# Pairs of attention scores at other slots of two FFN tiles, and the raw weights of plain tiles at other slots

## The chip, the core and the metric

The kernel runs on one core of a Trainium2 chip. A core has a tensor engine (PE in the profile, with its weight loads as PEld), a vector engine (DVE), a scalar engine (ACT), a general engine (POOL) and a queue that issues DMAs (SP). Each works through its own list of instructions in order and waits on semaphores for the others. The metric is the device time of one execution in microseconds: the median of several runs, lower is better. The trace is that of one profiled execution.

## The reference

One transformer block over a sequence of 2048 tokens of width 576, in float32. Attention has 32 query heads of 18 and one shared key and value head; the FFN is gated and bilinear, 4608 wide:

```python
scores = einsum("bhqd,bkd->bhqk", q, k) * Dh ** -0.5
p = softmax(scores); o = einsum("bhqk,bkd->bhqd", p, v)
h = x + merge(o) @ wo               # x layer-normed before wq, wk, wv
g, u = ln(h) @ w_gate, ln(h) @ w_up
out = h + (g * u) @ w_down
```

Float32 products are made of fp32r products: each operand is split into a high part and the rest, and three of the four cross products are added.

## The kernel before, in words

The sequence is cut into four query blocks of 512. After a prologue, and the attention of the first block, the FFN of blocks 0, 1 and 2 runs (`ffn`, 36 tiles of the hidden width each, 108 in all), and between its matmuls the attention of the next blocks is worked in. The FFN of the last block has code of its own (`last_block`).

**A tile of the FFN** is 27 *slots*, counted by `j`. A slot is one matmul of the gate into the PSUM bank `pg` and one of the up product into `pu` (L1035); each uses 64 of the 128 rows of the array, so the two run side by side. Then ACT copies `pg` into `hf` (L1062), and DVE multiplies it by `pu` (L1067). Two tiles, an even and an odd one, make a *pair of tiles*: from their two `hf`, `left_first`, `left` and `left_sums` make the operands of the down product by a Strassen-like scheme of seven products (splits on POOL and DVE, lines L96 and L97, tiles `S` and `room`); the 42 matmuls of it (`down`, L987) run at the end of the *next* even tile. Their results are added to `h` by DVE (L993), or by an ACT copy to `tmp` (L997) and a POOL addition (L998).

**A pair of scores** (`pair`, with `scores`) is two matmuls side by side into a PSUM tile `s` (L701) and one ACT exponential of 128x1024 into `P` (L702). There are two `s` tiles, so a pair needs the exponential of the pair two before it. An FFN tile takes eight pairs while there are any (`on`). `flush` multiplies all `P` that wait with the values (L706); it runs at the end of every even tile, ahead of `down`. The order of all instructions is that in which the Python code makes them; no scheduler moves them. The list `PAIRS` names the slots ahead of which a pair stands: its first entry for even tiles, its second for odd ones, its third for the last tile of a block.

**Where the pairs stand before the change.** Even tile: ahead of slots 0, 4, 8, 12, 16 and 20, and two after the copy to `hf`. Odd tile: ahead of 0, 4, 8, 12, 16, 20 and 24, and one after the copy to `hf`. Then comes the next even tile, whose slot 0 has a pair again.

**The PSUM banks** of `pg`, `pu`, the down product and the output projection are handed out in turn from a ring of three (`ps_r`). An odd tile takes two; the next even tile takes the third for its `pg`, and for its `pu` the bank that was `pg` of the odd tile. So the first `pu` matmul of that even tile waits for the copy of the odd tile's `pg` to `hf`.

**Weights.** `load_w(n)` issues the DMA of the raw gate and up weights of tile n (`wr`, one buffer, 576 KB), and `split_w(n)` makes the high and low parts (`ws`, two buffers): a POOL cast and a DVE subtraction. Since `wr` has one buffer, the load of n+2 waits for the split of n+1.

**Plain tiles.** When the pairs are used up, tiles are not `on`: 15 tiles at the end of the FFN of block 2. They hold no pairs, `split_w` stands at slot 3 and `load_w` at slot 9, `down` comes ahead of the copy to `hf`, and steps of `ahead`, which prepare the last block, stand at some slots (`AHEAD`).

**Heads.** When the eight key-value passes of a group of heads are done, the result goes through DVE and through DMAs (`ob<-ob`) into the layout that the output projection wants. `run_aux`, at the end of a tile and at slot 12, makes these steps; one of them is an ACT cast of `ob` into `room` (L96), which waits for those DMAs.

Of the kernel before, what the change touches and what calls it, by code (L numbers as in the profile page):

```python
# [57 lines left out]
class Block:  # L58
# [951 lines left out]
    def ffn(self, b):  # L1010
        pe, act, dve = self.pe, self.act, self.dve
        X, hid, todo = self.X, [], None
        ahead = self.ahead()
        if b == 0:
            self.sums = self.weight_sums()
            next(self.sums)
        for f in range(NF):
            n_ = NF * b + f
            k = f % 2
            w = self.ws.pop(n_)  # L1020
            on = self.more(b + 2)
            last = f == NF - 1 and b + 1 < NB
            end = b == NB - 2
            if on:
                pg, pu = self.ps_r(f"pg{n_}"), self.ps_r(f"pu{n_}")
            else:
                gu = self.ps_s(f"gu{n_}")
                pg, pu = gu[:, 0], gu[:, 1]
            j = 0
            for c in range(9):  # L1030
                for wk, xk in ((0, 0), (0, 1), (1, 0)):
                    if on and j in (PAIRS[2] if last else PAIRS[k]) and self.more(b + 2):
                        self.pair()
                    for o, ps in ((0, pg), (64, pu)):
                        pe.matmul(ps, w[o:o + 64, wk, c], X[o:o + 64, xk, c], start=(j == 0), stop=(j == 26))  # L1035
                    if j == (8 if on else 2) and todo and not plain(n_ - 2):
                        self.left_sums()
                    if j == 3:
                        self.split_w(n_ + 1)
                    if j == (14 if on else 9):  # L1040
                        self.load_w(n_ + 2)
                    if j == 5 and k:
                        self.left_first(n_ - 1, hid[0])
                    if j == 12:
                        self.run_aux(within=True)
                    if 0 < f < NF - 1 and j in (8, 16, 24) and self.sums:
                        if next(self.sums, "end") == "end":
                            self.sums = None
                            self.load_wd(self.n_wd + 2)
                    if j == 6 and last and not end:  # L1050
                        self.normal(b + 1)
                    if end and f == TURN - 1 and j == 12:
                        self.normed[NB - 1] = self.mv, self.rstd(self.mv[:, :, 1], "bl", self.nc.gpsimd)
                    if end and f in AHEAD and j in AHEAD[f]:
                        for _ in range(AHEAD[f][j]):
                            next(ahead)
                    j += 1
            if todo and not on:
                drain(self.down(b, *todo))
                self.load_wd(self.n_wd + 7)  # L1060
            hf = self.hh.tile([P, TB], F32, tag="hf", bufs=2, name=f"hf{n_}")
            act.copy(hf, pg)  # L1062
            if on and not last:
                for _ in range(1 if k else 2):
                    if self.more(b + 2):
                        self.pair()
            dve.tensor_tensor(hf, pu, hf, ALU.mult)  # L1067
            hid.append(hf)
            if k:
                self.left(n_ - 1, hid)  # L1070
                hid = []
            if end and f in TURNS:
                for _ in range(TURNS[f]):
                    next(ahead)
            if not k or last:
                self.flush(len(self.pend))
            if todo and on:
                drain(self.down(b, *todo))
                self.load_wd(self.n_wd + 7)
            if f < NF - 1:  # L1080
                self.run_aux()
            todo = (f // 2,) if k else None
        if end:
            del X, pg, pu, gu, w, ps, hf, self.X
            self.last_block(ahead, self.down(b, *todo))
            return
        both(self.spread(b + 1), self.down(b, *todo))
        self.load_wd(self.n_wd + 4)
        if b + 2 < NB:
            self.load_x(b + 2)  # L1090
# [500 lines left out]
ORDER = (0, 3, 4, 2, 5, 6, 1)  # L1591
WD_BUFS = 9
NTMP = 3
PAIRS = (range(0, 24, 4), range(0, 28, 4), range(0, 24, 3))
AHEAD = {30: {4: 1}, 31: {3: 1, 7: 1, 11: 1, 15: 1, 19: 1, 23: 1}, 32: {4: 1},
         33: {3: 1, 7: 1, 11: 1, 15: 1, 19: 1, 23: 1}, 34: {10: 1}, 35: {5: 1, 11: 1, 17: 1, 23: 1}}
TURNS = {28: 5, 29: 2}
# [16 lines left out]
def both(a, b):  # L1614

    live = [a, b]
    while live:
        live = [x for x in live if next(x, drain) is not drain]


def plain(n):

    return n % NF == NF - 2
# [28 lines left out]
def drain(gen):  # L1652
    for _ in gen:
        pass
# [85 lines left out]
```

## Time and profile before

| what | value |
|---|---|
| median of 3 runs | 2316.66 us (2316.43 to 2317.4) |
| the profiled execution | 2313.73 us |
| its span in the trace | 2311.9 us |
| busy: PE, DVE, ACT, POOL | 98%, 58%, 61%, 39% of the span |
| FFN tiles with pairs | 93, from 372 to 1807 us of the span |
| plain tiles | 15, from 1820 to 1985 us |

A row of a timeline gives start and length in us, engine, line, operation, output<-inputs, shapes, and how many equal instructions it merges; in brackets stands the idle time of the engine ahead of it and what ended that. A row of the chain of waits gives start, length, and the engine and line that set the end at that time. A row of a waits view gives who waited for whom, the total in us, how many times, and the longest.

### The profile page before, as it was taken

What the parts mean: (1) busy time and instruction counts of PE and PEld (TensorE: products, weight loads), DVE (VectorE), ACT (ScalarE), POOL (GpSimd) and SP (SyncE); (2) the same over time, 40 slices, a digit from 0 to 9 for tenths busy, and PEclk for the clock granted to TensorE, in tenths of its full rate; (3) what the DMA queues carried; (4) which work ended last, traced back from release to release, by engine and by line L of the source; (5) the groups of instructions that cost most, each with busy time, mean ns of one, the idle gap of its engine ahead of it and who ended that gap; (6) DMA issues with size and microseconds to landing.
All of it is one profiled execution on the core that took longest, in us unless ns stands there. A gap on an engine that the chain in (4) does not pass through costs nothing.

```text
span 2311.9 us, 45915 instructions
## 1 busy us (share of the span) xinstructions
PE 2258.3 (98%) x17972; PEld 1660.3 (72%) x17972; DVE 1347.6 (58%) x2184; ACT 1418.9 (61%) x1902; POOL 897.6 (39%) x979
## 2 busy tenths in 40 slices
PE   7999999999999999999999999999999999999999
PEld 5333345777777777677777777777777778999999
DVE  8565645554545555455555456554454667778876
ACT  7888877656566665566665656665656412455553
POOL 4445302444443453334444444433333345322222
PEclk9999999999999999999999999999999999999999
DMA  5879834545554554645554554654333435677775
GB/s 175 272 253 302 276 122 118 163 146 169 168 158 153 168 169 146 195 147 165 155 166 147 171 172 144 178 180 143 124 121 99 138 129 170 190 252 246 228 246 178
DMA packets 200433, 407.01 MB, mean 176 GB/s; under 512 B 22637, under 2 KB 54509, under 8 KB 200213
## 3 DMA queue, kind: packets, MB, share of 16 engines
q1 hardware_dynamic: 197621, 393.42, 53.4%
q0 software_dynamic: 2592, 10.62, 1.5%
q8 instruction: 143, 2.34, 0.4%
q14 instruction: 77, 0.63, 0.1%
HBM read 317.27 MB, written 74.55 MB: 169 GB/s over the span
## 4 chain that ended last, share of the span: by engine, by line
PE 77%; DVE 3%; ACT 3%; POOL 2%; issue 2%; DMA 1%; SPq 0%; ACTq 0%; POOLq 0%; DVEq 0%
PE pg L1035 16%; PE acc L706 15%; PE y L987 12%; PE s L701 8%; PE gs L1253 8%; PE pu L1035 6%; PE yq L1218 4%; PE yo L832 3%; ACT P L702 2%; PE gu L1035 2%; PE gs L1260 1%; DVE ws L97 1%; PE y L957 1%; POOL h L998 1%; POOL room L96 1%
## 5 line engine op out<-in xcount | busy, mean ns | idle before, releaser
L702 ACT ACTIVATE P<-s 128x1024 f32<-128x1024 f32 x1024 | 1017.2, 1029 | 221.6 <-PE s L701 135.1
L1035 PE MATMUL pu<-X,ws 64*128 64x512 f32 x2511 | 680.0, 392 | 0.0
L1035 PE MATMUL pg<-X,ws 64*128 64x512 f32 x2511 | 674.7, 389 | 0.1
L1035 PEld LDWEIGHTS pg<-X,ws 64*128 64x128 f32 x2511 | 462.7, 186 | 46.1 <-ACT tmp L964 0.4
L706 PE MATMUL acc<-P,V 128*32 128x512 f32 x4096 | 479.9, 597 | 0.1
L1035 PEld LDWEIGHTS pu<-X,ws 64*128 64x128 f32 x2511 | 460.2, 186 | 25.0 <-ACT hf L1062 7.9
L701 PE MATMUL s<-q,kT 56*128 56x512 f32 x2048 | 438.7, 421 | 19.8 <-ACT P L702 18.6
L998 POOL TENSOR_TENSOR h<-h,tmp 128x288 f32<-128x288 f32 x306 | 239.4, 811 | 383.7 <-ACT tmp L997 382.4
L997 ACT COPY tmp<-y 128x288 f32<-128x288 f32 x306 | 122.1, 399 | 392.5 <-PE y L987 350.8
L701 PEld LDWEIGHTS s<-q,kT 56*128 56x128 f32 x2048 | 203.7, 184 | 200.5 <-ACT P L702 153.2
L987 PEld LDWEIGHTS y<-wdo,room 128*128 128x128 f32 x2142 | 294.9, 191 | 56.5 <-issue 36.2
L987 PE MATMUL y<-wdo,room 128*128 128x288 f32 x2142 | 309.6, 303 | 14.4 <-DVE h L993 11.4
L993 DVE TENSOR_TENSOR h<-h,y 128x288 f32<-128x288 f32 x408 | 175.3, 451 | 217.6 <-PE y L987 217.6
L706 PEld LDWEIGHTS acc<-P,V 128*32 128x32 f32 x4096 | 114.5, 109 | 260.6 <-issue 255.8
L97 DVE TENSOR_TENSOR ws<-wr,ws 128x1152 fp32r<-128x1152 f32 x108 | 190.1, 1760 | 129.4 <-POOL ws L96 126.6
L96 POOL CAST room<-hf 128x256 fp32r<-128x256 f32 (+1 forms) x108 | 68.4, 633 | 336.8 <-DVE hf L1067 336.8
L96 POOL CAST ws<-wr 128x1152 fp32r<-128x1152 f32 x108 | 128.7, 1192 | 135.7 <-DMA wr<-in_wgu_dram 135.7
L1067 DVE TENSOR_TENSOR hf<-pu,hf 128x512 f32<-128x512 f32 x93 | 63.8, 686 | 198.5 <-ACT hf L1062 198.5
L1201 POOL TENSOR_TENSOR wsum<-wsum,wsum 128x512 f32<-128x512 f32 x72 | 146.5, 2034 | 47.9 <-DMA wsum<-in_wgs_dram 38.9
L717 DVE STREAM_TRANSPOSE os<-acc 128x512 f32<-128x512 f32 x32 | 22.9, 717 | 149.5 <-PE acc L706 149.5
L1035 PE MATMUL gu<-X,ws 64*128 64x512 f32 x810 | 94.5, 389 | 0.0
L97 DVE TENSOR_TENSOR room<-hf,room 128x256 fp32r<-128x256 f32 (+1 forms) x108 | 90.7, 840 | 2.9 <-POOL room L96 2.9
(262 smaller groups left out, 2776.4 us busy)
## 6 DMA issues: line engine op xcount, KB each, us to landing
wdo<-wd_dram SPq DMA_DIRECT2D x492, 288.0 KB
wr<-in_wgu_dram SPq DMA_DIRECT2D x108, 576.0 KB
wsum<-in_wgs_dram SPq DMA_DIRECT2D x108, 256.0 KB
wd_dram<-wd_room SPq DMA_DIRECT2D x20, 1008.0 KB
wsum_dram<-wsum SPq DMA_DIRECT2D x72, 256.0 KB
raw<-wsum_dram SPq DMA_DIRECT2D x72, 256.0 KB
q<-q_dram SPq DMA_DIRECT2D x64, 216.0 KB
raw<-in_wgs_dram SPq DMA_DIRECT2D x54, 256.0 KB
```

The source lines that it names most:

```text
L96: (copy or self.cast)(hi, src)
L97: self.dve.tensor_tensor(lo, src, f32(hi), ALU.subtract)
L701: self.pe.matmul(s_[:, i], self.kT[o:o + 56, t * P:(t + 1) * P], q[o:o + 56, pr], start=True, stop=True)
L702: self.act.activation(p_, s_, AF.Exp, scale=SCALE)
L706: self.pe.matmul(acc[32 * j:32 * j + 32, :], self.V[:, t, :], Ps[j // 2][:, j % 2, :], start=(t == 0), stop=(t == NT - 1), skip_group_chec ...
L987: pe.matmul(y[:, :HD], m[:, t * P:(t + 1) * P], k, start=(first and j == 0), stop=(j == 2), skip_group_check=True)
L993: dve.tensor_tensor(hs, hs, y[:, :HD], ALU.add)
L997: act.copy(z, y[:, :HD])
L998: pool.tensor_tensor(hs, hs, z, ALU.add)
L1035: pe.matmul(ps, w[o:o + 64, wk, c], X[o:o + 64, xk, c], start=(j == 0), stop=(j == 26))
L1201: pool.tensor_tensor(to, x, y, op)
L1253: pe.matmul(bank[:, g * HT:(g + 1) * HT], W[:, wk, c, g], X[:, 2 * xk + c], start=(first and g == c == wk == xk == 0), stop=(c == 1 and wk ...
```

## The change

Three edits. In tiles with pairs, the even tile has them ahead of slots 3, 7, 11, 14, 18 and 22 and two after the copy to `hf`, as before in number; the odd tile has them ahead of slots 0, 4, 8, 11, 15, 19, 23 and 26, and none after the copy. In the last tile of a block they stand ahead of 0, 3, 7, 10, 13, 17, 20 and 23 instead of 0, 3, 6, ..., 21. The number of pairs in each tile is the same. In plain tiles, `split_w` of an even tile moves from slot 3 to slot 9, and `load_w` of an odd tile from slot 9 to slot 3.

```diff
-                    if j == 3:
+                    if j == (3 if on or k else 9):
                         self.split_w(n_ + 1)
-                    if j == (14 if on else 9):
+                    if j == (14 if on else 3 if k else 9):
                         self.load_w(n_ + 2)
...
             act.copy(hf, pg)
-            if on and not last:
-                for _ in range(1 if k else 2):
-                    if self.more(b + 2):
-                        self.pair()
+            for _ in range(2 if on and not k else 0):
+                if self.more(b + 2):
+                    self.pair()
             dve.tensor_tensor(hf, pu, hf, ALU.mult)
...
-PAIRS = (range(0, 24, 4), range(0, 28, 4), range(0, 24, 3))
+PAIRS = ((3, 7, 11, 14, 18, 22), (0, 4, 8, 11, 15, 19, 23, 26), (0, 3, 7, 10, 13, 17, 20, 23))
```

What this does to the order of instructions is shown at three places. The first is ACT around the end of odd tile 11; `P1_3_11_1` is the exponential of the eighth pair of that tile, `hf11` the copy, `P1_3_12_0` the first exponential of even tile 12. Before:

```order
L702 ACTIVATE P1_3_11_0_12396<-s1_3_11_0_12395 128x1024 [waits PE_49]
L1062 COPY hf11_12408<-pg11_12306 128x512 [waits DVE_49,PE_49]
L702 ACTIVATE P1_3_11_1_12411<-s1_3_11_1_12410 128x1024 [waits PE_49]
L702 ACTIVATE P1_3_12_0_12425<-s1_3_12_0_12424 128x1024 [waits PE_49]
L702 ACTIVATE P1_3_12_1_12441<-s1_3_12_1_12440 128x1024 [waits PE_49]
```

With the change:

```order
L702 ACTIVATE P1_3_11_0_12394<-s1_3_11_0_12393 128x1024 [waits PE_49]
L702 ACTIVATE P1_3_11_1_12407<-s1_3_11_1_12406 128x1024 [waits PE_49]
L1062 COPY hf11_12413<-pg11_12306 128x512 [waits DVE_49,PE_49]
L702 ACTIVATE P1_3_12_0_12431<-s1_3_12_0_12430 128x1024 [waits PE_49]
L702 ACTIVATE P1_3_12_1_12447<-s1_3_12_1_12446 128x1024 [waits PE_49]
```

The exponential of the eighth pair has moved ahead of the copy.

The second place is PE at the same boundary, from the last slot of tile 11 to the first of tile 12. Before:

```order
L1035 MATMUL pg11_12306<-X0_10336,ws11_12100 128x512
L1035 MATMUL pu11_12307<-X0_10336,ws11_12100 128x512
L701 MATMUL s1_3_11_1_12410<-q1_3_11313,kT_86 128x512 [waits Activation_49]
L701 MATMUL s1_3_11_1_12410<-q1_3_11313,kT_86 128x512
L701 MATMUL s1_3_12_0_12424<-q1_3_11313,kT_86 128x512 [waits Activation_49]
L701 MATMUL s1_3_12_0_12424<-q1_3_11313,kT_86 128x512
L1035 MATMUL pg12_12422<-X0_10336,ws12_12321 128x512 [waits DVE_49,Pool_49]
L1035 MATMUL pu12_12423<-X0_10336,ws12_12321 128x512 [waits Activation_49]
```

With the change:

```order
L701 MATMUL s1_3_11_1_12406<-q1_3_11311,kT_86 128x512 [waits Activation_49]
L701 MATMUL s1_3_11_1_12406<-q1_3_11311,kT_86 128x512
L1035 MATMUL pg11_12306<-X0_10336,ws11_12100 128x512
L1035 MATMUL pu11_12307<-X0_10336,ws11_12100 128x512
L1035 MATMUL pg12_12422<-X0_10336,ws12_12321 128x512 [waits DVE_49,Pool_49]
L1035 MATMUL pu12_12423<-X0_10336,ws12_12321 128x512 [waits Activation_49]
```

The two pairs between the tiles are gone; one now stands a slot earlier, the other three slots later. The wait of `pu12` for ACT has stayed.

The third place is DVE in plain tile 104, around the subtraction of `split_w` for tile 105 (`XS5` belongs to `ahead`, the `h2` row to `down`). Before:

```order
L97 TENSOR_TENSOR room_10399<-S_10400,room_10399 128x1024
L97 TENSOR_TENSOR ws105_28426<-wr105_28363,ws105_28426 128x1152
L1146 TENSOR_TENSOR XS5_28200<-xsums_28205,XS5_28200 128x512
L993 TENSOR_TENSOR h2_16912<-h2_16912,y2_15_0_28480 128x288
L993 TENSOR_TENSOR h2_16912<-h2_16912,y2_15_1_28481 128x288
```

With the change:

```order
L97 TENSOR_TENSOR room_10399<-S_10400,room_10399 128x1024
L1145 TENSOR_TENSOR XS5_28197<-xsums_28202,XS5_28197 128x512
L97 TENSOR_TENSOR ws105_28440<-wr105_28347,ws105_28440 128x1152
L993 TENSOR_TENSOR h2_16912<-h2_16912,y2_15_0_28480 128x288
L993 TENSOR_TENSOR h2_16912<-h2_16912,y2_15_1_28481 128x288
```

The subtraction for `ahead` and that of `split_w` have changed places. The same happens in tile 102. These are the only moves on DVE; on SP and POOL no instruction has another place than before.

## The prediction

> **What bounds the kernel now.** I read the page's busy line and its chain by engine first, then the chain in order of time over one pair of FFN tiles, then PE's waits and the waits on the copy to `hf`, and last the timelines of PE and ACT at one boundary between tiles.
>
> ```profile
> PE 2258.3 (98%) x17972; PEld 1660.3 (72%) x17972; DVE 1347.6 (58%) x2184; ACT 1418.9 (61%) x1902; POOL 897.6 (39%) x979
> PE 77%; DVE 3%; ACT 3%; POOL 2%; issue 2%; DMA 1%; SPq 0%; ACTq 0%; POOLq 0%; DVEq 0%
> ```
>
> PE is the bound; ACT has time to spare on average. The chain in order of time, from one flush to the next:
>
> ```profile
> 1747.63 7.00 PE acc L706 x64
> 1754.64 5.89 PE y L987 x42
> ...
> 1767.91 1.03 ACT P L702
> ...
> 1777.57 7.00 PE acc L706 x64
> ```
>
> A pair of tiles takes 1777.57 - 1747.63 = 29.94 us. Apart from PE one row of another engine is in it: at 1767.91 an exponential, at the boundary from the odd tile to the next even one. PE's waits over all tiles with pairs, and who waits for the copy to `hf`:
>
> ```profile
> PE s L701 <- ACT P L702: 15.0, 48, 4.4
> ...
>   PEld pu L1035: 7.9, 44
> ```
>
> The first row is what pairs wait for exponentials. The last says that 44 times the weight load of a `pu` matmul waits for the copy. 44 is the number of boundaries from an odd tile with pairs to an even one: 17 in each of the first two FFN blocks, 10 in the third. One of them on PE:
>
> ```profile
> 1767.47 0.39 PE L701 MATMUL s<-q,kT 56*128 56x512 f32 x2
> ...
> 1767.93 0.39 PE L1035 MATMUL pg<-X,ws 64*128 64x512 f32 x1
> ...
> 1768.16 0.39 PE L1035 MATMUL pg<-X,ws 64*128 64x512 f32 x1
> ...
> 1768.39 0.39 PE L701 MATMUL s<-q,kT 56*128 56x512 f32 x2
> 1768.98 0.50 PE L701 MATMUL s<-q,kT 56*128 56x512 f32 x2 [0.20 <-ACT P L702]
> 1769.32 0.39 PE L1035 MATMUL pg<-X,ws 64*128 64x512 f32 x1
> 1769.46 0.49 PE L1035 MATMUL pu<-X,ws 64*128 64x512 f32 x1
> ...
> 1770.73 0.39 PE L1035 MATMUL pg<-X,ws 64*128 64x512 f32 x1
> ```
>
> and on ACT:
>
> ```profile
> 1767.91 1.02 ACT L702 ACTIVATE P<-s 128x1024 f32<-128x1024 f32 x1
> 1768.83 0.58 ACT L1062 COPY hf<-pg 128x512 f32<-128x512 f32 x1
> 1769.29 1.05 ACT L702 ACTIVATE P<-s 128x1024 f32<-128x1024 f32 x1
> ```
>
> A slot takes 1768.16 - 1767.93 = 0.23 us, a pair's scores as much. From the last slot (1768.16) to the even tile's first `pu` (1769.46) are 1.30 us, in which PE has a slot and two pairs to do, 0.69: 0.61 us are lost. To slot 4 (1770.73) 1.27 us pass for four slots and a pair, 1.15: another 0.12, since `pg` and `pu` no longer start together. So about 0.73 us of each 29.94 us is loss, all here: 44 x 0.73 = 32 us is all that another placing could win at these boundaries.
>
> **The change part by part.** *Odd tile's end: the dear part.* The eighth pair now stands ahead of slot 26, and its exponential ahead of the copy on ACT. With the rows above as steps: scores start at 0; the exponential starts 0.44 later (1767.47 to 1767.91; the one of slot 23, three slots and a pair, 0.92 us, earlier, lets ACT go at the same moment, since the copy followed its exponential after 0.92); the copy starts 0.92 after that (1767.91 to 1768.83); the first `pu` of the even tile 0.63 after that (1768.83 to 1769.46). Sum 0.44 + 0.92 + 0.63 = 1.99. PE without a wait would be there after one pair and one slot, 0.46. Lost: 1.53 instead of 0.61, so **+0.92 us a boundary**; the 0.12 stay. The trace has no copy behind an exponential that late, so both ends: 0, if ACT took the copy right behind the exponential of slot 23 (0.92 earlier, a stall of 0.61 as now); and at most +1.2, if exponential and copy did not overlap (0.44 + 1.03 + 0.58, and 0.05 from the copy's end, 1769.41, to `pu`: 2.10, less 0.46) and the 0.12 came twice. I take 0.92, since the steps are all rows of the same boundary and ACT works in order.
>
> Queued behind the waiting `pu` are all of PE's even tile; on ACT nothing is delayed but the copy. The `hf` of the odd tile comes later with it, and DVE's and POOL's Strassen work too, but that is wanted only by `down`, after 27 slots and 7.00 us of `acc`.
>
> *Even tile's pairs later.* Slots 3 to 22 instead of 0 to 20 give the exponential two slots more at the start and take from the 7 slots ahead of the closing two pairs: 5 slots are 1.15 us, an exponential 1.03, so no new wait. The closing pairs, the flush, `down` and the start of the odd tile stay as they are.
>
> *The casts of heads.* Twelve times ACT has a cast for the output projection between the two tiles:
>
> ```profile
> L96 ACT CAST room<-ob 128x512 fp32r<-128x512 f32 x12 | 7.5, 626 | 7.1 <-DMA ob<-ob 7.0
> ...
> 431.16 7.00 PE acc L706 x64
> 462.23 7.00 PE acc L706 x64
> ...
> 525.32 7.00 PE acc L706 x64
> 555.18 7.00 PE acc L706 x64
> 585.56 7.00 PE acc L706 x64
> ...
> 678.45 7.00 PE acc L706 x64
> 708.64 7.00 PE acc L706 x64
> ```
>
> Here the first two exponentials of the even tile queue behind it. Against 29.86 us (525.32 to 555.18) the pairs of tiles with a cast take 31.07, 30.38 and 30.19: 1.2, 0.5 and 0.3 us more. Ten boundaries have these three sizes, two, two and six of them: 5.2 us. With the change PE gets to slot 3 later and has no pair before it; the cast fits. I take **-5 us**, between 0 and -5.2. The eleventh, at tile 38, is longer:
>
> ```profile
> 958.91 0.62 ACT L96 CAST room<-ob 128x512 fp32r<-128x512 f32 x1 [4.30 <-DMA ob<-ob]
> ...
> 960.50 0.80 PE L701 MATMUL s<-q,kT 56*128 56x512 f32 x2 [4.42 <-ACT P L702]
> ```
>
> The third pair of the tile waits for the first exponential. It stands ahead of slot 8 now and of slot 11 then: PE has three slots more behind it when the DMA lands, and the boundary's own stall goes under. **-0.7** there instead of +0.92.
>
> *Last tiles.* 3 or 4 slots apart instead of 3: nothing to win but some 0.1 us each; left out.
>
> *Plain tiles.* Both moved steps stand where they stood on SP and POOL: between slots 3 and 9 nothing else is queued there. So the DMA of `wr`, the cast and the subtraction begin when they began. On DVE two rows change places in tiles 102 and 104. In tile 104:
>
> ```profile
> 1947.49 2.13 DVE L97 TENSOR_TENSOR room<-S,room 128x1024 fp32r<-128x1024 f32 x1 [0.94 <-POOL room L96]
> 1949.55 1.35 DVE L97 TENSOR_TENSOR ws<-wr,ws 128x1152 fp32r<-128x1152 f32 x1
> 1950.82 1.27 DVE L1146 TENSOR_TENSOR XS<-xsums,XS 128x512 fp32r<-128x512 f32 x1
> 1952.02 0.81 DVE L993 TENSOR_TENSOR h<-h,y 128x288 f32<-128x288 f32 x2
> ```
>
> Both run back to back, and PE waits for the `h` row behind them; in the other order it starts at the same time. **0**, between -1.3 and +1.3 (one of the two rows).
>
> **Sum.** 43 x 0.92 = 39.6; -0.7; -5: **+34 us**. Against the profiled execution 2313.73 + 34 = 2347.7; that lies 2.9 under the median of the runs shown, against which I predict 2316.66 + 34 = **2350.7**. With the upper bound 43 x 1.2 - 0.7 - 5 = +46, 2363; with 0.75 a boundary +26.5, 2343. The likeliest's own range is 2343 to 2363.
>
> **Rivals.** *Faster: an evenly spread row of pairs keeps ACT busy and PE never waits.* For it: the 15.0 us of waits for exponentials, which the change goes at. It needs the copy to be off PE's path: the first `pu` would have to find another bank, or the copy to end within 0.46 us of the last scores. Against it: the 44 waits of `pu`, one at each boundary, and the change leaves the ring of banks as it is. Price: 44 x 0.73 + 5 = 37 won, 2279. Chance 0.07.
>
> *No change.* The lower bound above: the copy goes ahead of the last exponential or costs what it costs now. Then 0 to -5, 2312 to 2317. Against it is the order on ACT. Chance 0.05.
>
> *The clock.* PE stands still for 1.53 us a boundary, 1.14 of it idle (the even tile's first `pg` still runs, 0.39). What idle time did to the granted clock (in the last three rows, of a view by windows, it is the third number from the right):
>
> ```profile
> 1913.12 0.67 PE L987 MATMUL y<-wdo,room 128*128 128x288 f32 x3 [2.09 <-ACT tmp L997]
> ...
> 1952.51 2.84 PE L987 MATMUL y<-wdo,room 128*128 128x288 f32 x14 [2.35 <-DVE h L993]
> ...
> 960.30:963.70 3.40, 3.20 (x16) 2.55 (x18) 0.00 (x0) 2.26 (x4) 0.92 (x1) 0.51 0.93 300
> 1913.00:1915.40 2.40, 2.27 (x17) 2.11 (x17) 1.22 (x3) 1.19 (x4) 2.40 (x4) 1.00 0.65 216
> 1953.60:1957.00 3.40, 3.40 (x16) 3.40 (x15) 0.52 (x2) 1.59 (x4) 2.44 (x4) 0.50 0.70 211
> ```
>
> After 2.09 us of idling the clock stayed at 1.00, after 2.35 and 4.42 it fell to 0.50 for 3.4 us, which costs 1.7. If 1.14 us were enough, 44 x 1.7 = 75 more: 2425. By the rows they are not. Chance 0.04. The Trainium skill's page "TensorE: Matmul & The Clock Gate", section "A second HAM failure mode: psum-queue depth-cycling", speaks for this rival: a kernel whose matmul groups idle briefly at each turn of the PSUM banks went to and fro between the two clocks. By that rule the change costs far more than the stall. The same page's first part puts the fall after an idle window of some 3.4 us; the fall after 2.35 here is earlier than that.
>
> *The plain tiles do win.* If the raw weights came sooner, part of this idling would go:
>
> ```profile
> L987 PE MATMUL y<-wdo,room 128*128 128x288 f32 x297 | 48.5, 323 | 13.5 <-DVE h L993 11.4 <-ACT tmp L997 2.1
> ```
>
> All 13.5 and three half-clock stretches of 1.7: 18.6 less, 2332 together with the +34. Against it: PE waits here for DVE and ACT, none of it for `wr`, and the queues stand as they stood. Chance 0.06.
>
> **How the numbers follow.** Likeliest 0.78, clock 0.04, plain tiles 0.06: slower by over 0.2% (4.6 us, about what a measurement of this kernel can tell from no change) 0.88; same 0.05; faster 0.07. The range, 2326 to 2364, takes in the likeliest's own, its bounds and the plain-tile rival; left out are the faster, the same and the clock rival, 0.16.
>
> **What would show it.** In the changed trace: on ACT the row of `hf<-pg` 0.92 us behind the start of an exponential at each odd tile's end, with no other between it and the even tile's first `pu`; `PEld pu` waiting for it 44 times with 1.1 us or more each, 50 us in all, instead of 7.9; waits of `s` for `P` down from 15.0 to about 5; a pair of tiles at 30.8 us; the plain stretch from 1820 to 1985 as long as before. The prediction is wrong if `pu` waits no longer than now, if the clock is 0.5 in tiles with pairs other than 38, or if the plain stretch changes by over 2 us.

## The result, and the profile after

The changed kernel takes 2346.0 us (median of 4 runs, 2344.61 to 2346.59) where the kernel before, run beside it, takes 2316.55 us (4 runs, 2315.48 to 2317.4). The ratio is 1.0127, with a 95% interval of 1.0109 to 1.0144: the change costs 29 us. 2350.7 was predicted. The profiled executions differ by 2346.18 - 2313.73 = 32.4 us, against the predicted sum of 34.

The page of the changed kernel, its busy line, its chain by engine and the group of `pu` matmuls, with that group before behind it:

```profile
PE 2252.1 (96%) x17972; PEld 1655.2 (71%) x17972; DVE 1344.5 (57%) x2184; ACT 1419.6 (61%) x1902; POOL 896.6 (38%) x979
...
PE 73%; DVE 4%; ACT 3%; issue 3%; POOL 3%; DMA 1%; SPq 0%; ACTq 0%; POOLq 0%; DVEq 0%
...
L1035 PE MATMUL pu<-X,ws 64*128 64x512 f32 x2511 | 694.9, 392 | 51.5 <-ACT hf L1062 51.4
```

```profile
L1035 PE MATMUL pu<-X,ws 64*128 64x512 f32 x2511 | 680.0, 392 | 0.0
```

PE works no longer than before (2252.1 us against 2258.3); it stands still for longer. Before, its `pu` group had 0.0 us of idle time ahead of it, now 51.5. PE's waits in the tiles with pairs:

```profile
PE pu L1035 <- ACT hf L1062: 51.4, 44, 1.4
PE s L701 <- ACT P L702: 2.8, 1, 2.8
```

and, from the view of the copy's line, who waits for it:

```profile
  PEld pu L1035: 70.0, 44
```

The waits of pairs for exponentials are gone but for one (15.0 us before, 48 times), and each of the 44 boundaries now has a wait of `pu` that averages 51.4 / 44 = 1.17 us. The 70.0 us are the wait of the weight loads ahead of these matmuls; PE itself still has the first `pg` to do in a part of it and stands idle for 51.4. One boundary, on PE:

```profile
1800.72 0.39 PE L701 MATMUL s<-q,kT 56*128 56x512 f32 x2
...
1802.71 0.50 PE L1035 MATMUL pu<-X,ws 64*128 64x512 f32 x1 [1.14 <-ACT hf L1062]
...
1803.05 0.40 PE L1035 MATMUL pu<-X,ws 64*128 64x512 f32 x1
...
1803.29 0.39 PE L701 MATMUL s<-q,kT 56*128 56x512 f32 x1
...
1803.53 0.40 PE L701 MATMUL s<-q,kT 56*128 56x512 f32 x1
```

on ACT, the exponential of slot 26 and the copy:

```profile
1801.16 1.02 ACT L702 ACTIVATE P<-s 128x1024 f32<-128x1024 f32 x1
1802.08 0.58 ACT L1062 COPY hf<-pg 128x512 f32<-128x512 f32 x1
```

and what the chain of waits has at this boundary and the one before, with the copy of the odd tile in it (the exponential that the chain names is that of slot 23):

```profile
1769.40 0.94 ACT P L702
...
1771.24 0.59 ACT hf L1062
...
1780.21 7.00 PE acc L706 x64
...
1800.23 0.94 ACT P L702
...
1802.08 0.59 ACT hf L1062
```

Scores at 1800.72, exponential at 1801.16, copy at 1802.08, `pu` at 1802.71: 0.44 + 0.92 + 0.63 = 1.99 us, the predicted steps. At all 44 boundaries the copy starts 0.92 us behind the start of the last exponential, and `pu` comes 1.99 to 2.25 us behind the last scores, 2.00 in the median. The last rows of PE show the skew: after the wait `pu` runs a slot behind `pg`, and so the first pair's two score matmuls, which run side by side elsewhere, start 0.24 us apart. Measured from the copy of one even tile to that of the next, an undisturbed pair of tiles lasts 30.8 us instead of 29.9, +0.93.

### The profile page after: what moved, and what is told of

Read it like the earlier page. It is cut to its first block, busy times and chain, and to the rows that moved or that the text cites. A ratio compares the mean times of both kernels' runs of the same rounds, so it can differ in the third digit from the quotient of the medians.

```text
span 2344.4 us, 45914 instructions
## 1 busy us (share of the span) xinstructions
PE 2252.1 (96%) x17972; PEld 1655.2 (71%) x17972; DVE 1344.5 (57%) x2184; ACT 1419.6 (61%) x1902; POOL 896.6 (38%) x979
## 4 chain that ended last, share of the span: by engine, by line
PE 73%; DVE 4%; ACT 3%; issue 3%; POOL 3%; DMA 1%; SPq 0%; ACTq 0%; POOLq 0%; DVEq 0%
PE pg L1035 16%; PE acc L706 15%; PE y L987 11%; PE s L701 8%; PE gs L1252 8%; PE pu L1035 5%; PE yq L1217 4%; PE yo L832 3%; ACT P L702 2%; PE gu L1035 2%; PE gs L1259 1%; POOL h L998 1%; ACT hf L1062 1%; DVE ws L97 1%; PE y L957 1%
## 5 line engine op out<-in xcount | busy, mean ns | idle before, releaser
L1035 PE MATMUL pu<-X,ws 64*128 64x512 f32 x2511 | 694.9, 392 | 51.5 <-ACT hf L1062 51.4
L1035 PE MATMUL pg<-X,ws 64*128 64x512 f32 x2511 | 693.8, 391 | 0.5 <-ACT tmp L964 0.5
L701 PE MATMUL s<-q,kT 56*128 56x512 f32 x2048 | 497.0, 415 | 7.5 <-ACT P L702 6.4
L701 PEld LDWEIGHTS s<-q,kT 56*128 56x128 f32 x2048 | 255.3, 184 | 169.5 <-ACT P L702 118.4
```

The costliest lines, as they stand in the source:

```text
L701: self.pe.matmul(s_[:, i], self.kT[o:o + 56, t * P:(t + 1) * P], q[o:o + 56, pr], start=True, stop=True)
```

## Experiments

Each kernel below computes all of the reference. What a pair of tiles gains or loses is measured as above, in the profile, against the kernel before.

### The eighth pair back behind the copy

The changed kernel, with one thing undone: the odd tile's eighth pair stands after the copy to `hf` again instead of ahead of slot 26.

```diff
-            for _ in range(2 if on and not k else 0):
+            for _ in range(0 if not on or last else 1 if k else 2):
-PAIRS = ((3, 7, 11, 14, 18, 22), (0, 4, 8, 11, 15, 19, 23, 26), ...)
+PAIRS = ((3, 7, 11, 14, 18, 22), (0, 4, 8, 11, 15, 19, 23), ...)
```

> The changed kernel, but the eighth pair of an odd tile stands behind the copy to hf again; all other slots as changed. Theory (the copy of the odd tile waits on ACT behind the last exponential, and the first pu of the even tile waits for the copy): last exponential ahead of the copy is that of slot 23, copy 1.36 us behind its scores, pu 1.99 behind them, PE there after 1.38: 0.61 us lost a boundary, as before the change; the casts of heads still fit. 2316.5 - 5 - 0.5 (tile 38) - 2 (plain) = 2309 us, the waits of the pu matmuls back to about 8 us. Rival (the denser pairs of the odd tile, 3 slots apart at two places, or the later pairs of the even tile cost the time): it stays within 10 us of 2346.

Measured: 2311.85 us (10 runs, 2308.58 to 2318.82); the kernel before, on the same chip, 2315.45; ratio 0.999 (0.9978 to 1.0002). The whole loss is gone, and with it the doubt about where it sits: one pair, 44 times, on the wrong side of a copy. (Of the 7.5 us that the expectation has below the kernel before, 3.6 are measured, and the interval takes in no change.) A typical pair of tiles is as long as before (+0.00), those with a cast of heads 0.2 to 0.5 us shorter. One part of the expectation missed. The waits of `pu` did not return to 8 us (PE's waits, then who waits for the copy):

```profile
PE pu L1035 <- ACT hf L1062: 10.9, 44, 0.3
PE s L701 <- ACT P L702: 3.8, 2, 3.6
```

```profile
  PEld pu L1035: 29.7, 44
```

The old loss was a wait of `s` for an exponential (15.0) and one of `pu` (7.9 on the weight loads) in turn. With no pair ahead of slot 0, PE reaches `pu` first, and the wait stands there instead. Its length is the same, so the even tile's own slots are neutral as long as the copy is where it was.

### The odd tile alone

The kernel before, with only the odd tile's eight slots changed and none behind the copy.

```diff
-                for _ in range(1 if k else 2):
+                for _ in range(0 if k else 2):
-PAIRS = (range(0, 24, 4), range(0, 28, 4), range(0, 24, 3))
+PAIRS = (range(0, 24, 4), (0, 4, 8, 11, 15, 19, 23, 26), range(0, 24, 3))
```

> The kernel before, with only the odd tile's slots changed (0, 4, 8, 11, 15, 19, 23, 26 and none behind the copy); even, last and plain tiles as before. Theory: pu comes 1.99 us behind the scores of slot 26, PE with one more pair at slot 0 of the even tile after 0.69: 1.30 lost instead of 0.61, 44 x 0.69 = 30 more, a part of the 5 us of the casts won: 2343 us (2340 to 2347). Rival (the even tile's later pairs cost it): 2317.

Measured: 2339.61 us (4 runs, 2338.58 to 2340.43), ratio 1.0108 (1.0091 to 1.0125), 0.4 us under the expected range; a typical pair of tiles +0.66 us against the 0.69 that the steps give.

PE's largest row of waits:

```profile
PE pu L1035 <- ACT hf L1062: 29.3, 44, 0.7
```

The even tile's pair ahead of slot 0 gives PE 0.23 us of work while it waits, so less is lost than in the full change. The two edits add up as the order of ACT's rows says they should: 0.66 of the 0.93 comes from the odd tile, the rest from taking that pair away.

### Spread evenly, and earlier

The changed kernel with the odd tile's pairs ahead of slots 0, 3, 7, 10, 13, 17, 20 and 23: as evenly spread, with the last one three slots sooner.

```diff
-PAIRS = ((3, 7, 11, 14, 18, 22), (0, 4, 8, 11, 15, 19, 23, 26), ...)
+PAIRS = ((3, 7, 11, 14, 18, 22), (0, 3, 7, 10, 13, 17, 20, 23), ...)
```

> The changed kernel, with the odd tile's eight pairs ahead of slots 0, 3, 7, 10, 13, 17, 20 and 23: still all ahead of the copy, but the last exponential is done when the last slot is. Theory: the copy starts 0.45 us after the start of the last pg, pu 0.63 after that, PE there after one slot, 0.23: 0.85 lost instead of 1.53, 44 x 0.68 = 30 less: 2316 us. Rival (dense pairs in the odd tile make PE wait): more pairs are three slots apart here, so 2346 or more.

Measured: 2320.83 us (10 runs, 2315.88 to 2324.89), ratio 1.0024 (1.0014 to 1.0034); a typical pair of tiles +0.26 us, where the steps give 0.85 - 0.61 = 0.24. The expected 2316 had left these 0.24 us out.

In PE's waits:

```profile
PE pu L1035 <- ACT hf L1062: 21.7, 44, 0.6
```

The price is the distance from the last scores to the copy; beyond it, evenness shows none. Three slots sooner give back 0.67 of the 0.93 us.

### The plain tiles' edits alone

> The kernel before with only the two edits in plain tiles. The changed kernel's trace has the pair of plain tiles 104 and 105 2.05 us shorter: PE's idle time ahead of the down product is 1.80 instead of 2.35 us, and no half clock follows. Theory (the two DVE rows that changed places: the one for ahead now runs while POOL is idle, 0.68 instead of 1.27 us): idle 1.8 us at that place, 0.55 us won for certain and 1.5 more where the half clock stays away; 2313.5 to 2315.5, nothing else moves. Rival (my prediction's step: the order of the two does not matter): 0.

```diff
-                    if j == 3:
+                    if j == (3 if on or k else 9):
-                    if j == (14 if on else 9):
+                    if j == (14 if on else 3 if k else 9):
```

Measured: 2313.78 us (10 runs, 2312.32 to 2316.48), before 2315.34; ratio 0.9994 (0.9985 to 1.0004). The time alone can't tell 1.5 us from nothing; the trace can. The stretch with tile 104's work is 2.05 us shorter, as in the changed kernel (whose difference to before goes from +34.4 to +32.4 us there), and nothing else in the plain tiles moves by more than 0.1. DVE in tile 104 of this kernel:

```profile
1948.02 2.13 DVE L97 TENSOR_TENSOR room<-S,room 128x1024 fp32r<-128x1024 f32 x1 [0.94 <-POOL room L96]
1950.07 0.68 DVE L1146 TENSOR_TENSOR XS<-xsums,XS 128x512 fp32r<-128x512 f32 x1
1950.68 1.34 DVE L97 TENSOR_TENSOR ws<-wr,ws 128x1152 fp32r<-128x1152 f32 x1
1951.94 0.81 DVE L993 TENSOR_TENSOR h<-h,y 128x288 f32<-128x288 f32 x2
```

Before, the same `XS` row took 1.27 us in the second place and the `ws` row 1.35 in the first. Swapped, the short one takes 0.68 and the `h` row stands 3.92 instead of 4.53 us behind the first of these rows. The reason is POOL, whose addition began just then. Before:

```profile
1950.72 0.82 POOL L998 TENSOR_TENSOR h<-h,tmp 128x288 f32<-128x288 f32 x1 [2.17 <-ACT tmp L997]
```

and in this kernel:

```profile
1951.22 1.46 POOL L998 TENSOR_TENSOR h<-h,tmp 128x288 f32<-128x288 f32 x1 [2.14 <-ACT tmp L997]
```

Before, POOL started first (1950.72) and DVE's row, due at 1950.82, lost 0.6 us to it; now DVE's `ws` row is under way when POOL starts, and POOL's addition loses 0.64 instead. POOL's result is wanted later, DVE's at once. So the one that starts second waits for most of what the other still has to run (0.59 of 0.72 us, 0.64 of 0.80), and the order of rows decides which that is. The Trainium skill's page "SBUF — State Buffer", section "SBUF: two separate sides", says that VectorE and GpSimd share a pair of ports under an exclusive lock, which whoever starts first holds for its whole instruction; both pairs of durations agree.

### A flush at the odd tile's end, too

If PE loses 0.73 us a pair of tiles at one boundary because ACT has not caught up, work that needs no ACT could stand there. The `acc` matmuls are such work: the kernel before does all of them at the even end. Here the odd end does those that are ready.

```diff
             if not k or last:
                 self.flush(len(self.pend))
+            elif on:
+                self.flush(len(self.pend) - 1)
```

> The kernel before, with a flush at the end of every odd tile with pairs too: all waiting P but the last key tile's (24 matmuls with the values, some 2.6 us) stand between the odd tile's last pair and the even tile's first slot, taken from the flush at the even tile's end; no work is added. Theory: the copy is done behind them and the 0.73 us of loss a boundary goes: 44 x 0.73 = 32, the casts' 5, and at tile 38 2.6 us of work go under the wait for the heads, which ends its half clock too (4): 2275 us (2270 to 2284). Rival (the loss at the boundary is ACT's or the order's, not a wait that other PE work can fill): 2312 to 2317.

Measured: 2291.33 us (4 runs, 2288.53 to 2292.22), ratio 0.9895 (0.9878 to 0.9912): 24 us faster than before, but above the expected 2270 to 2284. The waits at these boundaries are gone; the first rows of PE's waits, with no `pu` among them:

```profile
PE y L987 <- DVE h L993: 5.8, 2, 3.0
PE s L701 <- ACT P L702: 2.6, 1, 2.6
```

Yet a pair of tiles is shorter by 0.40 us, not 0.73. The boundary on PE:

```profile
1653.72 0.42 PE L701 MATMUL s<-q,kT 56*128 56x512 f32 x2
1654.08 2.78 PE L706 MATMUL acc<-P,V 128*32 128x512 f32 x24
1656.79 0.50 PE L701 MATMUL s<-q,kT 56*128 56x512 f32 x2
1657.12 0.39 PE L1035 MATMUL pg<-X,ws 64*128 64x512 f32 x1
```

From scores to `acc` are 0.36 us instead of 0.23, the 24 `acc` rows take 2.71 instead of 24 x 7.00 / 64 = 2.63, and from scores to `pg` are 0.33 instead of 0.23: together 0.31 us. PE has no idle time in these rows; it goes from one shape of matmul to another and back. The expectation had left that out.

### The changed kernel with the same flush

> The changed kernel, with the flush at the end of odd tiles of the run before (all waiting P but the last key tile's). Theory: the 2.6 us of matmuls with the values stand between the odd tile's last slot and the even tile's first pu, so the copy behind the last exponential is done in time, and what the change lost goes together with what the kernel before lost: as in the run before, a pair of tiles 0.4 us under that of the kernel before (0.33 us of the gain go for entering and leaving the flush once more), 2290 us (2286 to 2294). Rival (the changed slots cost time by themselves): it stays above the run before by a good part of the 30 us that the change cost.

```diff
+            elif on:
+                self.flush(len(self.pend) - 1)
```

Measured: 2290.42 us (4 runs, 2288.48 to 2293.99), ratio 0.9897 (0.9881 to 0.9914). With this cover at the boundary, the order that cost 29 us costs nothing: a pair of tiles is 0.37 us shorter than before, as in the kernel before with the flush (0.40). So, to within these 0.03 us, the pairs' spread acts on a pair of tiles only through this one wait. This and the previous kernel are the fastest of the study and can't be told apart: 1.0% under the kernel before, 2.3% under the changed one.

### The flush moved instead of added

If going in and out again costs 0.3 us, the flush may be moved to the odd end whole. So that a group of heads ends at an odd tile, eight more pairs go ahead of the first FFN, and one tile more is plain.

```diff
-            if not k or last:
+            if on and (k or f == NF - 2):
                 self.flush(len(self.pend))
...
-            while self.n_pair % 8 != 4:
+            while self.n_pair % 32 != 28:
```

> The kernel before, with the flush of the tiles with pairs moved as a whole from the end of even tiles to the end of odd tiles (and once at the end of the tile before the last of a block), and eight more pairs ahead of the first FFN block, so that a group of heads ends at an odd tile; one tile more is plain for that. Theory: all 7 us of matmuls with the values stand at the boundary, the copy is done behind them, and no flush is entered once more: 0.73 a boundary, 32 us, less some 3 for pairs done outside the FFN: 2285 us (2278 to 2295), below the run with two flushes. Rival (the even tile's end, now without a flush between its copy and the down product, gives a wait of its own): above 2291.

Measured: 2316.87 us (10 runs, 2314.75 to 2323.73), ratio 1.0009 (0.9999 to 1.0018). The gain is gone; the rival was right. The wait moved to the even end, which the flush had covered (two rows of PE's waits):

```profile
PE y L987 <- ACT hf L1062: 6.6, 27, 0.3
PE y L987 <- DVE hf L1067: 5.0, 13, 0.4
```

Without `acc` ahead of it, `down` comes straight behind the closing pairs, and it takes all three banks of the ring, two of which the even tile's `pg` and `pu` have just used. PE's idle time in these rows is only 0.29 us for each of the 40 waits, but the loss is larger: from the last closing scores to `down` pass 0.64 us (median) instead of the 0.23 of a pair, and `down`, which waits again for its second bank, lasts 6.16 instead of 5.88. Together that is 0.41 + 0.28 = 0.69 us, about the 0.73 that had been lost at the other end. Each end needs work of its own that owes ACT nothing.

### A third flush

To see whether the 0.3 us is the price of each going in and out, one more flush, in the middle of the even tile, on top of the added one.

```diff
                     if j == 12:
                         self.run_aux(within=True)
+                    if j == 13 and on and not k:
+                        self.flush(len(self.pend) - 1)
```

> The kernel before with the added flush at the odd tile's end and with one more flush in the middle of the even tile (ahead of slot 14, all but the last pair that waits), so that TensorE goes into the acc matmuls and out of them once more in each pair of tiles; the number of acc matmuls is the same. Theory: going into acc and out again costs a fixed 0.33 us whatever the number of matmuls, which is why the flush at the odd end won 0.40 us and not 0.73. Then 46 pairs of tiles with 0.33 more: 2291.3 + 15 = 2306 us (2302 to 2310), and nothing newly waits. Rival: the 0.33 belongs to the odd end alone (scores right ahead of the flush, or what is left of the wait for the copy), and a flush among the slots costs nothing: 2291 us, within 3.

Measured: 2323.64 us (7 runs, 2322.66 to 2324.91), ratio to before 1.0031 (1.0019 to 1.0042). That is 32 us above the kernel with the added flush, twice the expected 15. A pair of tiles is 0.78 us longer than there. At the new flush PE has

```profile
1660.36 0.39 PE L701 MATMUL s<-q,kT 56*128 56x512 f32 x2
...
1661.13 1.92 PE L706 MATMUL acc<-P,V 128*32 128x512 f32 x16
1662.99 0.50 PE L1035 MATMUL pg<-X,ws 64*128 64x512 f32 x1
...
1663.56 0.39 PE L701 MATMUL s<-q,kT 56*128 56x512 f32 x2
```

1663.56 - 1660.36 = 3.20 us for a pair, four slots and 16 `acc` rows, 5 x 0.23 + 16 x 0.109 = 2.90. So 0.30 us is the fixed price, among slots as well as beside scores: this part of the theory held. The other half is a wait that the expectation denied ("nothing newly waits"). The closing flush has 24 rows left, and they take 3.14 us instead of 2.63, since the exponentials of the closing pairs are not done:

```profile
PEld acc L706 <- ACT P L702: 28.1, 94, 0.3
```

That row is from the weight loads' waits; this is the timeline, in which 3.14 lies between the two starts:

```profile
1667.11 3.21 PE L706 MATMUL acc<-P,V 128*32 128x512 f32 x24
1670.25 2.01 PE L987 MATMUL y<-wdo,room 128*128 128x288 f32 x13
```

### A flush of the smallest size

```diff
             elif on:
-                self.flush(len(self.pend) - 1)
+                self.flush(1)
```

> The kernel before with a flush of one pair alone (four acc matmuls, 0.44 us) at the odd tile's end, in place of seven pairs; the others stay for the flush at the even end. Theory of the fixed cost: 0.44 us of work and the 0.33 of going in and out again are longer than the 0.61 us that the first pu waits, so the wait is gone and the gain is the same 0.40 us a pair of tiles: 2291 us, within 3. Rival: only the acc matmuls themselves cover the wait; 0.61 less 0.44 stay, 0.17 a boundary, which is 44 times 0.17 = 7.5 us more: 2299 us.

Measured: 2296.44 us (4 runs, 2295.52 to 2298.86), ratio 0.9917 (0.99 to 0.9933). The time is between the two expectations, and the trace decides. The expectation had a size wrong: an entry of the list that waits is two pairs, eight `acc` rows, and PE spends 1.00 us on it, so the cover was twice as long as meant, and the rival (0.17 us left over) was not put to the test. At the boundaries it does what the longer flush does: no `pu` waits, and a typical pair of tiles lasts 29.51 us against 29.49. The 4 us by which its span is longer (2293.7 against 2289.8) arise elsewhere, at the ends of blocks above all: from tile 34 to tile 38 it gains nothing on the kernel before where the longer flush gains 3.8 us, from 92 to 94 1.1 instead of 2.6, and some of that comes back in other tiles. What the last flush of a block gains from fewer rows was not followed up.

## Why the prediction was right

**Odd tile's end.** 0.92 a boundary was predicted, +0.93 measured; 1.99 us from scores to `pu` was predicted and is what the rows show. Both bounds are refuted by the rows: ACT did take the exponential ahead of the copy, and the copy started 0.92 us behind the start of the exponential, not after its end. The first experiment shows that this one move carries the whole loss, the second and third that its size follows the steps to 0.03 us. The weight loads of `pu` waited longer than the 50 us that the prediction named for them (70.0); 50 fits PE's own idle time, 51.4.

**The 0.12 us of skew stay.** They do, in another place: `pu` still runs behind `pg`, and now the first pair's scores start apart too.

**The casts of heads.** -5 was predicted. The ten boundaries with a cast lengthen by 0.45 us on average instead of 0.93, so -4.8. **Tile 38:** -0.7 predicted, -0.57 measured.

**Even tile's pairs later: no new wait.** Right; the one wait of `s` that is left is 2.8 us long. The **last tiles** of the first two blocks, left out at 0.1 us each, cost 0.3 each.

**Plain tiles: 0.** This step is wrong: "in the other order it starts at the same time". I took the two DVE rows' durations as their own, and the longer `XS` row was long only because POOL's addition had started ahead of it. Swapped, PE's idle time ahead of `down` falls from 2.35 to 1.80 us, and the half clock behind it does not come: 2.05 us in all, just over the 2 us that the prediction had set as its limit. It is also outside what the bounds meant (one row, 1.3), because the clock was not in them.

**The clock rival** is refuted: 44 idle times of 1.14 to 1.40 us, one every 31 us, and the clock in the tiles with pairs stays at 1.00 (third number from the right) apart from tile 38, where the trace has its only half-clock stretch between 380 and 1850 us:

```profile
380.00:970.00 590.00, 568.85 (x4699) 419.63 (x4697) 304.23 (x460) 365.13 (x453) 246.78 (x244) 1.00 0.50 158
990.00:1850.00 860.00, 829.06 (x6848) 610.28 (x6847) 435.90 (x665) 528.80 (x657) 335.00 (x343) 1.00 0.47 146
```

The Trainium skill's rule on matmul groups that idle briefly at each turn of the PSUM banks ("TensorE: Matmul & The Clock Gate", section "A second HAM failure mode: psum-queue depth-cycling") is not borne out for idle times of this length.

**The sum.** 43 x 0.92 - 0.7 - 5 = 34 predicted. The difference of the two traces behind the last tile with pairs is +34.4, and less 2.05 in the plain tiles +32.4, which is also what the profiled executions differ by. That it meets the 34 so closely is in part luck: the 44 boundaries alone add up to 33.0 of the predicted 33.9, and the other 1.4 come from places that the prediction left out (0.6 ahead of the first copy, 0.3 and 0.3 in the two last tiles, 0.2 where the pairs end). The medians differ by 3 us less, since the profiled execution of the kernel before (2313.73) lay 2.8 us under the median of its runs and that of the changed kernel at its own.

**What another placing could win.** The prediction had 32 us. None of the placings of pairs tried here won it. Other work at that place won 0.40 of the 0.73 us of a pair of tiles; the rest is the price of going in and out of the `acc` matmuls. (The 24 us of the whole kernel also hold gains at the casts of heads and at the ends of blocks.)

## What to carry to other kernels

On an engine that works in order, spreading its tasks evenly is not the aim: ask which of its results TensorE wants next, and let nothing stand ahead of that one. Where a wait can't be moved, put work there that needs nothing from the engine that is late, and count what it costs to switch to it and what the place that it came from had been covering. A duration from a trace belongs to its neighbours as well; before two rows change places, see who ran beside each.

## What the runs showed of the hardware that was not expected

**A half clock after short idle times, but not always.** The prediction read that 2.09 us of idling keep the clock and 2.35 lose it. That is no threshold. In the first experiment's kernel a gap of 2.82 us kept the clock and one of 1.78 lost it. PE's rows behind these gaps:

```profile
1863.98 2.27 PE L987 MATMUL y<-wdo,room 128*128 128x288 f32 x15 [2.82 <-DVE h L993]
...
1950.23 4.17 PE L987 MATMUL y<-wdo,room 128*128 128x288 f32 x19 [1.78 <-DVE h L993]
```

and the windows behind them (the granted clock is the third number from the right):

```profile
1951.20:1954.60 3.40, 3.40 (x16) 3.40 (x15) 0.64 (x2) 1.54 (x4) 2.31 (x3) 0.50 0.93 331
1864.00:1867.40 3.40, 3.40 (x25) 3.40 (x26) 1.49 (x4) 1.60 (x4) 1.73 (x3) 1.00 0.88 303
```

In the changed kernel it is the other way round. The same two views of it:

```profile
1898.57 1.75 PE L987 MATMUL y<-wdo,room 128*128 128x288 f32 x8 [2.82 <-DVE h L993]
...
1986.34 4.71 PE L987 MATMUL y<-wdo,room 128*128 128x288 f32 x33 [1.80 <-DVE h L993]
```

```profile
1986.40:1989.80 3.40, 3.40 (x25) 3.40 (x26) 1.50 (x4) 1.60 (x4) 1.94 (x4) 1.00 0.84 283
1899.30:1902.70 3.40, 3.40 (x16) 3.40 (x15) 0.88 (x2) 1.19 (x3) 2.23 (x3) 0.50 0.65 214
```

So of the 2.05 us in tile 104, some 0.57 are the swap of the two rows, and about 1.5 are the clock's: in three kernels of the study with the same swap whose clock did fall there, the tile gained 0.56 to 0.58.

What decides is, for the most part, where the gap falls. In each of the eleven traces the half-clock stretches between 380 and 2050 us start a whole number of steps of 3.413 us from one another (before, the starts are 960.34, 1837.56, 1864.87 and 1953.62: 257, 8 and 26 steps), and they last one step or two. What counts is how long PE idles within one step. Two steps of the first experiment's kernel, the second of them right ahead of its fall (PE's busy time stands behind the comma, the clock third from the right):

```profile
1862.42:1865.83 3.41, 1.85 (x14) 1.00 0.73 250
1947.76:1951.17 3.41, 1.63 (x13) 1.00 0.13 20
```

and two of the changed kernel, the first right ahead of its fall:

```profile
1895.87:1899.28 3.41, 0.71 (x5) 1.00 0.41 131
1984.61:1988.03 3.42, 1.69 (x12) 1.00 0.31 90
```

The gap of 2.82 us that kept the clock lies across the end of a step: 1.26 us fall into one and 1.56 into the next. The 2.82 that lost it lie almost whole in one step, 2.70. In the eleven traces together, 32 steps at full clock had 1.80 us or more of idle time, and a half-clock step followed each of them; 5,282 had less than 1.50, and none was followed by one. Of the 16 in between, 5 were: 1.78 us lost the clock in three kernels, 1.73 and 1.79 kept it in two others. What decides there is open. The waits of 1.1 to 1.4 us at the boundaries lie under all of this, wherever they fall. The Trainium skill's page "TensorE: Matmul & The Clock Gate", section "What's actually happening", has a free-running window of 3413 ns, and the steps agree with it. The same section puts the fall after at least one idle window of that length; here some half of one is enough, and the measurement decides. A change that moves a plain tile by a microsecond can win or lose 1.5 us in this way, which limits how far a difference of 2 us of such kernels can be read.

**Going in and out of the `acc` matmuls.** 0.30 to 0.33 us each time, whatever their number: 0.30 by the rows with 16 (the third flush), 0.31 by those with 24, and 0.73 - 0.40 = 0.33 by the gain of a pair of tiles, with 24 rows as with 8. What in the switch takes this time is not shown.
